# VectorE's weight roundings in two parts, weights used one step later, and one plain token chunk in place of two, in a fused attention and MLP kernel

## The chip, the cores and the metric

The kernel runs on one core of a Trainium2 chip. The metric is the time of one execution on the device, in microseconds (us). Engines are named as the profile names them: PE is TensorE, PEld its weight loads, DVE is VectorE, ACT ScalarE, POOL GpSimd, SP SyncE. A ratio is the mean time of one kernel's fast runs over the mean of the other kernel's fast runs in the same rounds, so it is not quite the ratio of the medians that are quoted beside it. Below 1 is faster than the kernel before.

## The reference, cut to what matters

```python
def _attn_ref(q, k, v, tau):                      # q, k, v: (8, 8, 576, 64)
    scores = scale * np.matmul(q, k.transpose(0, 1, 3, 2))
    thresh = np.max(scores, axis=-1, keepdims=True) - tau
    scores = np.where(scores >= thresh, scores, -1000000000.0)
    attn = np.exp(scores - np.max(scores, axis=-1, keepdims=True))
    attn = attn / (np.sum(attn, axis=-1, keepdims=True) + 1e-09)
    return np.matmul(attn, v)

def _moe_ref(x, w_in, w_out):                     # x: (4608, 512), d_ff 2048
    r = np.maximum(x @ w_in, 0.0)
    return (r * r) @ w_out
```

The weights arrive as 64-bit floats and are rounded to 32 bits on the chip. That is the work that the change moves.

## The kernel before

Work goes in *steps*. A step takes one block of 128 query rows of a pair of heads: scores on TensorE (L200), the row maximum on VectorE (L205), exponentials on ScalarE (L216), the masks on VectorE (L228), the division on GpSimd (L240), and for blocks of earlier steps transposes and the product with v on TensorE. VectorE works in the order in which the program issues. There are two score buffers, and the masks free them, so TensorE's next scores wait for masks.

Weights come in 32 *pieces* of rounding (16 of w_in, 16 of w_out). One piece takes two operations on ScalarE, three on VectorE and two on GpSimd:

```python
        elif stage == 1:
            nc.vector.tensor_scalar(out=tu, in0=hi, scalar1=0x80000000, ...)          # L137
            nc.vector.scalar_tensor_tensor(out=tu, in0=eu, scalar=3, in1=tu, ...)     # L138
            nc.vector.tensor_scalar(out=eu, in0=tu, scalar1=0xFF800000, ...)          # L140
        elif stage == 2:
            nc.gpsimd.tensor_tensor(out=d, in0=d, in1=e, op=ALU.mult)                 # L142
        else:
            nc.gpsimd.tensor_tensor(out=weight_piece(i)[1], in0=..., in1=..., op=ALU.add)   # L144
```

The plan of how many pieces each step rounds is the following; from step 20 on, `i == NBLK` is every fifth step: 24, 29, 34.

```python
        if s < HP * FIRST:                        # steps 0 to 7
            x = int(n > 0 and i == 0)
        else:
            x = 2 if n >= 2 * HP and i == NBLK else 1
```

In a step the order on VectorE is maximum, `round_weights(now[0], 1)` (L137, L138, L140), masks; in the last step of a pair of heads (24, 29 and 34 among them) the next q and k are transposed before the masks, and the rounding stands behind the masks. A second piece of the same step runs whole at the end of the step, in front of the next step's maximum.

TensorE fills its time between attention parts with *pieces* of the MLP, one of 1.76 us by the program's count, taken from a queue as soon as the weights they need are rounded:

```python
    def fill(us):
        state["left"] += us
        while waiting and state["left"] >= PIECE_US / 2 and waiting[0][0] <= state["rounded"]:
            ...                                   # issue the piece
```

The MLP runs on 18 chunks of 256 tokens. The first two (`PLAIN = 2`) use 16 plain output pieces each (L399, 4 records a piece); all later ones use seven products in 14 pieces (L431), which multiply with sums of quarters of w_out. The 16 subtractions that make these sums (L390, VectorE) stand one behind each input piece of chunk 2:

```python
        if j == PLAIN:
            posts.append(lambda: sum_quarters(x))
```

Their slots are the same memory in which raw weights are staged and the third slot of attention weights lies. The last rounding is in step 34, and the program lets no sum be made before step 37.

## Time and profile before

| | kernel before |
|---|---|
| time, median of 3 runs | 1431.7 us (1430.45 to 1433.82) |
| profiled execution | 1435.75 us, span 1434.0 us |
| TensorE idle in the whole span | 50.6 us |
| TensorE's waits, 100 to 250 us | 15.2 us, 7.0 of them for the last rounding (L144) |

The table of stretches for three stretches; the columns are the stretch, its length, the busy time of PE, PEld, DVE, ACT, POOL with instruction counts, the granted TensorE clock, the DMA share and GB/s:

```profile
20.00:60.00 40.00, 34.40 (x229) 25.49 (x230) 31.87 (x73) 23.56 (x59) 20.88 (x29) 0.87 0.64 124
100.00:250.00 150.00, 134.75 (x932) 89.68 (x932) 118.16 (x226) 87.17 (x210) 109.53 (x125) 0.94 0.39 100
250.00:440.00 190.00, 188.44 (x942) 133.90 (x941) 120.23 (x249) 53.95 (x135) 94.34 (x125) 1.00 0.47 86
```

Between 100 and 250 us, where most weights are rounded, TensorE is idle for 15.25 us and its clock is 0.94. From 250 us on it is idle for 1.56 us.

### The profile page before, as it was taken

The page shows a single profiled execution, that of the slowest core. Times are in us where ns is not written, and L with a number is a line of the kernel's source. Part 1 is how long each engine was busy: PE and PEld are TensorE (multiplying, and loading weights), DVE is VectorE, ACT ScalarE, POOL GpSimd, SP SyncE. Part 2 cuts the span into 40 slices and gives each one's busy share as a digit, 9 for nine tenths or more (in the row PEclk, how much of TensorE's full clock was granted, in tenths as well). Part 3 has the DMA queues.
Part 4 walks back from the last instruction along what each step waited for, and adds up shares of the span by engine and source line. Part 5 has one row for each costly group of instructions (what it writes and reads, how often), then busy time and mean ns, then how long its engine had stood idle before and what let it go on. Part 6 is the DMA issues. An engine that isn't in the chain of part 4 may idle for free.

```text
span 1434.0 us, 21996 instructions
## 1 busy us (share of the span) xinstructions
PE 1383.4 (96%) x7412; PEld 1055.1 (74%) x7412; DVE 853.3 (60%) x1770; ACT 435.5 (30%) x1064; POOL 708.4 (49%) x928
## 2 busy tenths in 40 slices
PE   5899988999999999999999999999999999999998
PEld 3676555747787777777777777778777777788887
DVE  5898875557756665756665657566657566621011
ACT  3765654323222323232222222223223232210100
POOL 3688766426454545354545435555454354531321
PEclk9999999999999999999999999999999999999999
DMA  7554442345544554454545544544555545430000
GB/s 149 126 139 122 111 103 53 63 78 102 91 91 92 106 101 93 79 106 88 98 87 106 96 91 89 105 87 91 91 109 89 94 87 104 77 73 15 1 15 15
DMA packets 503823, 125.93 MB, mean 88 GB/s; under 512 B 494912, under 2 KB 495712, under 8 KB 503712
## 3 DMA queue, kind: packets, MB, share of 16 engines
q1 hardware_dynamic: 494448, 107.42, 40.8%
q0 software_dynamic: 6880, 16.82, 3.8%
q8 instruction: 60, 0.98, 0.3%
q10 hardware_dynamic: 2384, 0.30, 0.1%
q14 instruction: 51, 0.42, 0.1%
HBM read 48.63 MB, written 9.44 MB: 40 GB/s over the span
## 4 chain that ended last, share of the span: by engine, by line
PE 86%; DVE 7%; issue 2%; ACT 2%; POOL 2%; DMA 1%; SPq 1%; DVEq 0%; POOLq 0%; ACTq 0%
PE bank L368 35%; PE bank L431 23%; PE s L200 12%; PE bank L319 11%; PE bank L399 3%; DVE w L228 1%; DVE st L205 1%; DVE turned L138 1%; PE bank L258 1%; DVE turned L137 1%; DVE turned L289 1%; ACT wT L259 1%; DVE turned L140 0%; DVE wo L228 0%; DMA wo<-in_moe_w_in_dram 0%
## 5 line engine op out<-in xcount | busy, mean ns | idle before, releaser
L368 PE MATMUL bank<-xT,w_in_sb 128*128 128x256 f32 x2304 | 521.4, 383 | 1.8 <-ACT osb L406 1.2
L368 PEld LDWEIGHTS bank<-xT,w_in_sb 128*128 128x128 f32 x2304 | 433.1, 190 | 82.7 <-issue 21.3
L205 DVE TENSOR_REDUCE st<-s 128x1 f32<-128x576 f32 x288 | 206.9, 753 | 323.5 <-PE s L200 323.3
L240 POOL TENSOR_SCALAR w<-w,st 128x576 f32<-128x576 f32 x269 | 236.6, 887 | 28.6 <-DVE st L231 22.1
L228 DVE SCALAR_TENSOR_TENSOR w<-s,st,w 128x576 f32<-128x576 f32 x269 | 207.5, 804 | 72.1 <-ACT w L216 72.0
L431 PE MATMUL bank<-wo,gsum 128*128 128x256 f32 x1024 | 234.0, 381 | 1.4 <-DVE u_sum L446 1.4
L379 POOL TENSOR_TENSOR g<-g 128x512 f32<-128x512 f32 x144 | 149.6, 1040 | 155.2 <-ACT g L378 131.5
L431 PEld LDWEIGHTS bank<-wo,gsum 128*128 128x128 f32 x1024 | 192.6, 190 | 36.4 <-issue 7.2
L200 PE MATMUL s<-kT,qT 64*128 64x288 f32 x1024 | 175.9, 439 | 27.3 <-DVE w L228 10.2
L238 POOL TENSOR_SCALAR st<-st 128x2 f32<-128x2 f32 (+1 forms) x160 | 38.0, 238 | 324.6 <-DVE w L228 311.2
L216 ACT ACTIVATE w<-s,st 128x576 f32<-128x576 f32 x269 | 184.9, 733 | 0.2 <-ACT st L214 0.2
L319 PE MATMUL bank<-wT,vs 128*64 128x128 f32 (+3 forms) x1700 | 178.6, 358 | 4.1 <-ACT wT L259 3.4
L431 PE MATMUL bank<-wo,g 128*128 128x256 f32 x768 | 178.7, 383 | 2.1 <-DVE osb L450 2.1
L431 PEld LDWEIGHTS bank<-wo,g 128*128 128x128 f32 x768 | 143.8, 190 | 31.6 <-issue 8.2
L200 PEld LDWEIGHTS s<-kT,qT 64*128 64x128 f32 x1024 | 99.4, 190 | 91.4 <-issue 66.6
L289 DVE STREAM_TRANSPOSE turned<-w 128x576 f32<-128x576 f32 x225 | 162.1, 754 | 3.5 <-POOL w L240 3.5
L319 PEld LDWEIGHTS bank<-wT,vs 128*64 128x64 f32 x1700 | 105.4, 140 | 74.8 <-issue 23.2
L378 ACT ACTIVATE g<-bank 128x512 f32<-128x512 f32 x144 | 86.2, 599 | 200.8 <-PE bank L368 200.8
L213 ACT ACTIVATE st<-st 128x2 f32<-128x2 f32 (+1 forms) x160 | 33.3, 208 | 324.9 <-DVE st L205 324.1
L333 ACT COPY xT<-bank 128x256 f32<-128x256 f32 x42 | 15.6, 372 | 279.8 <-PE bank L319 279.8
L444 DVE TENSOR_TENSOR gsum<-g 128x512 f32<-128x512 f32 x32 | 20.8, 681 | 107.3 <-PE bank L431 107.3
L399 PE MATMUL bank<-wo,g 128*128 128x512 f32 x128 | 62.1, 620 | 7.3 <-POOL wo L144 7.0
(69 smaller groups left out, 944.6 us busy)
## 6 DMA issues: line engine op xcount, KB each, us to landing
wT<-turned SPq DMA_DIRECT2D x800, 72.0 KB, 2.2
ql<-in_q_dram SPq DMA_DIRECT2D x126, 72.0 KB, 2.5
wo<-in_moe_w_in_dram SPq DMA_DIRECT2D x16, 512.0 KB, 4.7
wo<-in_moe_w_out_dram SPq DMA_DIRECT2D x16, 512.0 KB, 3.7
out_dram<-osb POOLq DMA_DIRECT2D x32, 256.0 KB, 2.7
vs<-in_v_dram POOLq DMA_DIRECT2D x50, 128.0 KB, 3.5
kl<-in_k_dram SPq DMA_DIRECT2D x63, 72.0 KB, 2.5
kl<-in_k_dram SPq DMA_DIRECT2D x63, 64.0 KB, 2.3
```

Source lines behind the costliest of these rows:

```text
L200: nc.tensor.matmul(sc[u][:, half, 0:HALF], lhsT, kT[rows, half * HALF:(half + 1) * HALF], start=True, stop=True)
L205: nc.vector.tensor_reduce(out=mx[:, u:u + 1], in_=sc[u][:, :, 0:HALF], axis=AX.XY, op=ALU.max)
L216: nc.scalar.activation(out=w[:, u, :].rearrange("p (h k) -> p h k", h=2), in_=sc[u][:, :, 0:HALF], func=AF.Exp, bias=bias[:, u:u + 1], sca ...
L228: nc.vector.scalar_tensor_tensor(out=wu, in0=sc[u][:, :, 0:HALF], scalar=thr[:, u:u + 1], in1=wu, op0=ALU.is_ge, op1=ALU.mult, accum_out=s ...
L240: nc.gpsimd.tensor_scalar(out=w[:, u, :], in0=w[:, u, :], scalar1=z[:, u:u + 1], scalar2=rcp[:, u:u + 1], op0=ALU.add, op1=ALU.mult)
L289: nc.vector.transpose(wb[:, u * KB:(u + 1) * KB, i % 2, :], w[:, u, :].rearrange("p (k q) -> p k q", q=32))
L319: nc.tensor.matmul(ps[u * D:(u + 1) * D, 0:nq], vs[n % 2][:, u * (NBLK + 1) + c, :], wT[:, cw, cols], start=(c == 0), stop=(c == NBLK))
L368: nc.tensor.matmul(h[:, x % 2, :], w_in_sb[:, c, f * P:(f + 1) * P], xT[:, c, at:at + TCH], start=(c == 0), stop=(c == NMC - 1))
L378: nc.scalar.activation(out=to, in_=h, func=AF.Relu)
L379: nc.gpsimd.tensor_tensor(out=to, in0=to, in1=to, op=ALU.mult)
L399: nc.tensor.matmul(o[t].rearrange("p (h d) -> p h d", h=2), g[:, f, t * P:(t + 1) * P], mov, start=(f == 0), stop=(f == NFT - 1))
L431: nc.tensor.matmul(to, left[:, f, :], wo[:, slot, f, :], start=(f == 0), stop=(f == HF - 1))
```

## The change

Its intent is threefold. *Split*: the third VectorE operation of a rounding (L140) goes behind the masks, so that the masks, which free the score buffers, come earlier. *Delay*: a rounded weight counts as usable only from the next step on, so that TensorE doesn't stand waiting for it. *Products*: `PLAIN = 1`, so chunk 1 too is done in 14 product pieces; the sums it needs are then made in steps 37 to 39. Cut to its core (asserts, the renumbered stages and the bodies of unchanged functions are left out):

```diff
+        elif stage == 2:
             nc.vector.tensor_scalar(out=eu, in0=tu, scalar1=0xFF800000, scalar2=None, op0=ALU.bitwise_and)
-        elif stage == 2:
+        elif stage == 3:
             nc.gpsimd.tensor_tensor(out=d, in0=d, in1=e, op=ALU.mult)
@@ mlp_in
-        if j == PLAIN:
-            posts.append(lambda: sum_quarters(x))
+        if j == PLAIN and state["step"] > first_dma + 1:
+            posts.append(lambda: some_sums(2))
@@ product
+        if sums:
+            some_sums(16 if x > 1 else 8)
@@
-    PLAIN = 2
+    PLAIN = 1
@@ fill
-        while waiting and state["left"] >= PIECE_US / 2 and waiting[0][0] <= state["rounded"]:
+        while waiting and state["left"] >= PIECE_US / 2 and waiting[0][0] <= state["usable"]:
@@ the loop over steps
+        state["usable"] = rounded_by[-1]
+        rounded_by.append(state["rounded"])
@@ before the masks
                 round_weights(now[0], 1)
-                round_weights(now[0], 2)
@@ behind the masks
+            if now:
                 round_weights(now[0], 2)
+                round_weights(now[0], 3)
```

## The prediction

> **What bounds the kernel now.** I read the page first, then the table of TensorE's waits, then the table of stretches, then the timeline around the longest waits. On the page, parts 1, 2 and 5:
>
> ```profile
> PE 1383.4 (96%) x7412; PEld 1055.1 (74%) x7412; DVE 853.3 (60%) x1770; ACT 435.5 (30%) x1064; POOL 708.4 (49%) x928
> PE   5899988999999999999999999999999999999998
> ...
> PEclk9999999999999999999999999999999999999999
> ...
> L399 PE MATMUL bank<-wo,g 128*128 128x512 f32 x128 | 62.1, 620 | 7.3 <-POOL wo L144 7.0
> ```
>
> TensorE is busy for 1383.4 of 1434.0 us, so all idle time together is 50.6 us, and most of it lies in the first seven or eight slices, while weights are being rounded. No change of waits alone can make 2% (28.6 us) unless it empties that stage. What TensorE waits for in the whole trace:
>
> ```profile
> PE s L200 <- DVE w L228: 11.9, 9, 3.5
> PE s L200 <- DVE kT L179: 9.3, 3, 8.4
> PE s L200 <- DVE wo L228: 7.7, 5, 3.0
> PE bank L399 <- POOL wo L144: 7.0, 5, 2.6
> ```
>
> Scores (L200) wait for VectorE's masks (L228), because the masks free the two score buffers: 19.6 us. Output products (L399) wait for freshly rounded weights (L144): 7.0 us. The table of stretches prices a long wait further:
>
> ```profile
> core 0: us, PE busy (x) PEld busy (x) DVE busy (x) ACT busy (x) POOL busy (x), PEclk, DMA share, GB/s
> 198.00:202.40 4.40, 1.78 (x15) 1.06 (x13) 4.26 (x6) 1.91 (x6) 4.10 (x5) 0.93 0.88 254
> 202.40:208.80 6.40, 6.40 (x27) 3.53 (x28) 4.97 (x9) 1.27 (x3) 5.46 (x6) 0.52 0.91 183
> 133.00:142.00 9.00, 9.00 (x34) 6.65 (x36) 8.08 (x15) 3.15 (x8) 7.03 (x9) 0.62 0.78 169
> ```
>
> After the 2.62 us wait at 199.8 us the clock is 0.52 for 6.4 us, so another 6.4 x 0.48 = 3.1 us is lost. After the 1.73 us wait at 131.3 us it is 0.62 for 9 us: 3.4 us. After the 2.12 us wait at 170.1 us the same view gives 0.77 for 7.3 us: 1.7 us. The three cost 8.2 us of work beyond their own length.
>
> **What sets a step while weights are rounded.** From the timeline at 219 us:
>
> ```profile
> 218.64 1.27 POOL L144 TENSOR_TENSOR wo<-turned 128x512 f32<-128x512 f32 x1
> 218.72 1.47 DVE L137 TENSOR_SCALAR turned<-wo 128x512 uint32<-128x512 uint32 x1
> 220.30 0.69 DVE L138 SCALAR_TENSOR_TENSOR turned<-turned 128x512 uint32<-128x512 uint32 x1
> 221.03 0.43 DVE L140 TENSOR_SCALAR turned<-turned 128x512 uint32<-128x512 uint32 x1
> 221.37 0.81 DVE L228 SCALAR_TENSOR_TENSOR w<-s,st,w 128x576 f32<-128x576 f32 x1
> 221.60 1.28 POOL L142 TENSOR_TENSOR turned<-turned 128x512 f32<-128x512 f32 x1 [1.69 <-DVE turned L140]
> ```
>
> L137 takes 0.42 us alone and 1.47 us here, ending just after GpSimd's L144. The masks start when L140 is through. Seen from the end M of the masks: L144 ends at M+3.5, L137 at M+3.8, L138 at M+4.6, L140 at M+5.0, the next masks at M+6.6. L142 starts at 215.12, 221.60 and 228.07 us, 6.5 us apart: a closed loop of VectorE and GpSimd, and TensorE, with 5.9 to 6.2 us of work in such a step with one MLP piece, is only just as long.
>
> **What the Trainium skill says.** "SBUF — State Buffer", section "SBUF: two separate sides": a VectorE operation with two SBUF inputs or in a two-port mode and a GpSimd operation exclude each other for the whole instruction. The trace agrees for L137 and L138 against L142 and L144 (0.42 to 1.47 us, 0.69 to 1.58 us). [...]the weight sums (L390) have a median of 0.68 us where the one-tensor L140 of as many elements takes 0.43. "TensorE: Matmul & The Clock Gate", section "Part 1: The HAM clock gate": after an idle window of about 3.4 us the array runs at half rate. The trace shows the half rate, but after holes of 1.7 to 2.6 us; the 1.66 us hole at 238.6 us did not trip it. The measured holes are what I use.
>
> **The change, part by part.**
>
> (a) *Chunk 1 by seven products.* The bookkeeping of the program, followed by hand, gives 14 product pieces for 16 plain output pieces. A plain piece is 4 records, and the chain has x16 in 7.06 us, so 16 pieces take 28.3 us. The chain has 112 records of L431, one chunk's 14 pieces, in 24.17 us, up to 24.8 where interrupted. Saved: 28.3 - 24.5 = 3.8 us of TensorE work. All of it is on the path.
>
> (b) *L140 after the masks.* 32 instructions leave the stretch between maximum and masks. The masks then need the exponentials and L138 only. In the new loop L140 runs at M+0.4, L142 ends at M+2.2, L240 at M+4.1, L144 at M+5.4; L137 starts at M+2.5 and no longer meets L144; the exponentials end at M+4.2 and the masks at about M+5.7. The loop falls from 6.5 to 5.7 us, below TensorE's step. Of TensorE's waits for masks I take off what L140, or L138 held by GpSimd, added at each: 0.4 at 39.7 us, 0.4 at 61.9, 0.8 at 68.0, 0.3 at 78.5, 0.9 at 133.0, 1.4 at 172.2, 0.4 at 222.3. Sum 4.6 us. The first waits (3.5, 3.0 and 2.1 us) have no rounding in front of them and stay.
>
> (c) *Weights a step later.* The five waits on L144 (7.0 us) and the one of L368 (0.6) go. But the 2.62 us one lies in step 30, where the second rounding of step 29 holds the maximum back to 200.33 us and the masks can't end before about 206: it comes back as a wait for masks. Net 5.0 us. Against that, the bookkeeping shows fewer pieces to fill holes: none in steps 17 and 21 (before: 1 and 3), one in most of the rest; at the end of step 35 31 pieces are done (before 36), then 12 come at once in step 36. The late pieces are not lost, since TensorE runs without a break afterwards, but holes open: step 17 has 4.3 us of work in a 5.7 us loop (1.4 us), step 21 has 3.4 us (2.3 us). New: 3.7 us.
>
> (d) *The sums of weights.* Before, 16 subtractions were spread over six steps of chunk 2. In the changed order 4 stand in front of step 38's maximum, 2 between it and the masks, and 10 in one row in front of step 39's. Step 38: I get masks about 1.0 us after TensorE wants them. Step 39: from the end of step 38's masks 0.35 + 10 x 0.68 + maximum 0.76 + two transposes 1.43 + mask 0.82 + 0.35 + the transposes of q and k 1.5 = 12.0 us until the next scores can start; TensorE has 1.0 us of scores and 4 pieces of 1.78, with the start 7.4 us after those masks. Hole: 4.6 us. Sum 5.6 us.
>
> (e) *Clock.* Before 8.2 us. After, long holes in steps 21, 30 and 39, some 3 us each: 9.0. Change +0.8.
>
> Sum: -3.8 - 4.6 - 5.0 + 3.7 + 5.6 + 0.8 = -3.3 us; 1431.7 - 3.3 = 1428.4, say 1428.5 us.
>
> **Rivals.** *Sums cost nothing* (TensorE is late enough in steps 37 to 39, or the throttle lets the hole pass): then -3.3 - 5.6 - 3 = -12 us, 1420. For it: before, step 44 holds three sums and TensorE waits only 0.40 us. Against: there they were three, here ten. *The holes of the delay win*: if steps 17, 20, 21 and 30 each lose a clock window and GpSimd, whose L240 now starts 1.5 us later after the masks, makes the transposes wait (before, the transposes waited for GpSimd hardly at all), 6 us more: 1434 to 1436. For it: GpSimd is 88% busy from 100 to 140 us. *TensorE hides all of it*: from 250 us on it has no idle time worth naming (4.2 us in 400 to 1200), so only (a) counts: 1428.
>
> **Range and chances.** The terms that could go wrong are (d) with its share of (e), about 8 us, and the holes of (c), about 6 us; in quadrature with a spread of runs of 1430.45 to 1433.82 this gives some 8 us to either side. The floor of all idle time makes 2% faster (1403) nearly impossible, and 2% slower (1460) would need a stall that nothing here shows.
>
> **What would show it.** Right: L399 x64 and L431 x1904 records; no wait on L144 over 0.5 us; L142's starts about 6 us apart in place of 6.5; a hole of TensorE for kT or masks of 3 to 5 us behind the row of ten sums, with a lowered clock after it; busy time of TensorE 3 to 4 us down except for clock. Wrong: no hole there (then faster, near 1420), or waits of L258 for GpSimd's L240 (then slower), or L140 in its new place meeting L142 of another piece and holding the next maximum.

## More of the kernel before

The profiled execution is slower than all three timed ones.

In the first stretch the clock was 0.87 in this execution: 40 x 0.13 = 5.2 us of clock.

Line numbers after the first hunk are one higher in the changed kernel, later ones up to seven: L200 is L201, L228 is L229, L140 is L141, L142 is L143, L144 is L145, L240 is L241, L390 is L393, L399 is L403, L431 is L438. In the variants with a changed choice of PSUM banks L403 is L406 and L438 is L441.

## The result, and the profile after

The changed kernel takes 1437.62 us (median of 4 runs, 1437.34 to 1438.55). The kernel before took 1431.43 us in the same rounds. The ratio is 1.0042, 95% interval 1.0024 to 1.0059: slower by 0.4%. That is within the 2% that the prediction was nearly certain of, but outside its range (1428.5 with some 8 us to either side, so about 1420 to 1436), and of the opposite sign. The output is correct.

From the page of the changed kernel, part 1:

```profile
PE 1378.8 (96%) x7460; PEld 1064.8 (74%) x7460; DVE 857.1 (60%) x1781; ACT 435.8 (30%) x1063; POOL 722.2 (50%) x933
```

TensorE works 4.6 us less than before (1378.8 against 1383.4) and the span is 1.9 us longer, so it is idle for 57.1 us, 6.5 us more. The same three stretches as above:

```profile
20.00:60.00 40.00, 33.91 (x239) 24.96 (x239) 32.65 (x74) 24.59 (x61) 20.89 (x29) 0.91 0.66 128
100.00:250.00 150.00, 134.65 (x945) 91.36 (x942) 118.82 (x236) 88.96 (x215) 116.50 (x128) 0.94 0.39 101
250.00:440.00 190.00, 183.23 (x965) 141.77 (x965) 120.65 (x242) 49.41 (x121) 97.36 (x125) 0.99 0.44 81
```

Two things are read from it. In the stage of the roundings nothing was won: 15.25 us of idle time before, and now 15.35, with the same clock of 0.94. And from 250 to 440 us, where there was hardly any idle time, there are 6.77 us in place of 1.56. What TensorE waits for from 100 to 250 us in the changed kernel (line and waiter, releaser, us in total, times, longest us):

```profile
PE s L201 <- DVE w L229: 7.5, 4, 3.9
PE s L201 <- DVE wo L229: 2.9, 1, 2.9
PE bank L403 <- ACT g L379: 2.0, 1, 2.0
PE bank L369 <- ACT osb L410: 1.6, 1, 1.6
```

In the kernel before the same view had 7.0 us for the last rounding (L144; the line stands in the prediction), 4.2 us for masks and nothing long for ScalarE:

```profile
PE s L200 <- DVE w L228: 2.1, 2, 1.7
PE s L200 <- DVE wo L228: 2.1, 1, 2.1
```

Now no wait for the rounding is left, as the delay intends, and 10.4 us for masks (7.5 + 2.9; wo is the third slot of attention weights, which lies in that memory) and 3.6 us for ScalarE stand in its place. The idle time changed its name.

(A hole is named by the step whose masks the scores of the next step wait for.) Where it is longest, in step 30, the timeline of VectorE in the changed kernel reads (start us, us, engine, line, operation):

```profile
195.84 0.82 DVE L229 SCALAR_TENSOR_TENSOR w<-s,st,w 128x576 f32<-128x576 f32 x1 [0.24 <-ACT w L217]
...
199.45 0.47 DVE L137 TENSOR_SCALAR turned<-wo 128x512 uint32<-128x512 uint32 x1
200.02 1.58 DVE L138 SCALAR_TENSOR_TENSOR turned<-turned 128x512 uint32<-128x512 uint32 x1
201.63 0.43 DVE L141 TENSOR_SCALAR turned<-turned 128x512 uint32<-128x512 uint32 x1
201.98 1.41 DVE L206 TENSOR_REDUCE st<-s 128x1 f32<-128x576 f32 x2
...
205.86 0.81 DVE L229 SCALAR_TENSOR_TENSOR w<-s,st,w 128x576 f32<-128x576 f32 x1
```

And TensorE's at the same place:

```profile
206.82 1.77 PE L201 MATMUL s<-kT,qT 64*128 64x288 f32 x4 [3.92 <-DVE w L229]
```

Step 29 rounds two pieces, both behind its masks; the first one's operations (196.97 to 199.54) are left out at the first "...". The three of the second piece (199.45 to 202.06) come on top, between the masks of step 29 (195.84) and the maximum of step 30 (201.98). From masks to masks it takes 10.0 us, and TensorE, with one MLP piece in the step, stands still for 3.92 us. From 206 to 212 us its clock is 0.50. Step 25, behind step 24 with two pieces, looks alike (2.95 us).

The second new hole, in the timeline of the changed kernel, VectorE, GpSimd and TensorE:

```profile
279.39 10.00 DVE L393 TENSOR_TENSOR wo<-wo 128x512 f32<-128x512 f32 x10
279.65 4.42 POOL L241 TENSOR_SCALAR w<-w,st 128x576 f32<-128x576 f32 x2 [0.26 <-DVE st L232]
285.58 1.59 POOL L358 TENSOR_TENSOR gsum<-g 128x512 f32<-128x512 f32 x1
287.23 5.35 PE L438 MATMUL bank<-wo,gsum 128*128 128x256 f32 x16 [4.08 <-POOL gsum L358]
294.10 1.24 PE L201 MATMUL s<-kT,qT 64*128 64x288 f32 x8 [1.52 <-DVE kT L180]
```

The ten sums in a row take 1.00 us each in the mean; the median of all 16 is 0.68. Beside them GpSimd's two divisions take 4.42 us; two of them took 1.63 us elsewhere (at 216.31 us). So GpSimd's sum of g (L358) is late, TensorE waits 4.08 us for it, and another 1.52 us for the transposed k, which VectorE reaches only behind the row.

The part that worked is seen in steps 32 to 35. VectorE's timeline of the changed kernel:

```profile
220.17 0.81 DVE L229 SCALAR_TENSOR_TENSOR w<-s,st,w 128x576 f32<-128x576 f32 x1
...
222.05 0.41 DVE L141 TENSOR_SCALAR turned<-turned 128x512 uint32<-128x512 uint32 x1
```

L141 now follows the masks, and the next step's masks start at 225.60 us, 5.4 us later, where the loop took 6.5 us before.

**How far the difference of 6 us is real.** Fifty-three executions of the kernel before were timed. They lie between 1430.31 and 1436.18 us, with a mean of 1433.0. The records of the 49 of them that list a clock order them:

| mean granted clock of the execution | executions | mean time |
|---|---|---|
| 0.990 to 0.991 | 10 | 1435.5 us |
| 0.993 to 0.995 | 25 | 1432.9 us |
| 0.996 to 0.999 | 14 | 1431.7 us |

The four that stand beside the changed kernel were on the quick side (mean 1431.8). Against the mean of all 53 the changed kernel, whose four runs have a clock of 0.990 to 0.992, is 4.8 us slower, or 0.33%. So 1.2 us of the 6 come from which executions of before were caught, and a comparison of the two profiled executions (1434.0 and 1435.9 us) shows only 1.9 us, since the profiled one of before was one of its slowest.

### The profile page after: what moved, and what is told of

Same layout as the page of the kernel before. It is cut to its first block, busy times and chain, and to the rows that moved or that the text cites. A ratio compares the mean times of both kernels' runs of the same rounds, so it can differ in the third digit from the quotient of the medians.

```text
span 1435.9 us, 22123 instructions
## 1 busy us (share of the span) xinstructions
PE 1378.8 (96%) x7460; PEld 1064.8 (74%) x7460; DVE 857.1 (60%) x1781; ACT 435.8 (30%) x1063; POOL 722.2 (50%) x933
## 4 chain that ended last, share of the span: by engine, by line
PE 79%; DVE 9%; SPq 5%; issue 3%; ACT 2%; DMA 1%; POOL 1%; DVEq 0%; POOLq 0%; ACTq 0%
PE bank L369 33%; PE bank L438 22%; PE s L201 12%; PE bank L320 10%; DVE w L229 2%; SPq L301 2%; SPq L308 2%; PE bank L403 2%; DVE st L206 1%; PE bank L259 1%; DVE turned L138 1%; DVE turned L290 1%; DVE wo L393 1%; SPq L162 1%; ACT w L217 1%
## 5 line engine op out<-in xcount | busy, mean ns | idle before, releaser
L438 PE MATMUL bank<-wo,gsum 128*128 128x256 f32 x1088 | 251.8, 384 | 5.8 <-POOL gsum L358 4.5
L241 POOL TENSOR_SCALAR w<-w,st 128x576 f32<-128x576 f32 x269 | 241.1, 904 | 27.4 <-DVE st L232 19.6
L229 DVE SCALAR_TENSOR_TENSOR w<-s,st,w 128x576 f32<-128x576 f32 x269 | 207.6, 804 | 75.8 <-ACT w L217 75.7
L438 PEld LDWEIGHTS bank<-wo,gsum 128*128 128x128 f32 x1088 | 205.3, 191 | 45.8 <-issue 9.6
L201 PE MATMUL s<-kT,qT 64*128 64x288 f32 x1024 | 178.6, 441 | 38.3 <-DVE w L229 17.2
L438 PE MATMUL bank<-wo,g 128*128 128x256 f32 x816 | 189.5, 382 | 0.9 <-DVE osb L457 0.9
L438 PEld LDWEIGHTS bank<-wo,g 128*128 128x128 f32 x816 | 153.1, 190 | 30.5 <-issue 6.9
L201 PEld LDWEIGHTS s<-kT,qT 64*128 64x128 f32 x1024 | 101.3, 191 | 95.8 <-issue 66.6
L334 ACT COPY xT<-bank 128x256 f32<-128x256 f32 x42 | 15.7, 373 | 281.4 <-PE bank L320 281.4
L184 POOL COPY qmid<-qT 64x64 f32<-64x64 f32 x64 | 18.3, 286 | 103.7 <-DVE qT L180 101.8
```

What stands on the lines that cost most here:

```text
L201: nc.tensor.matmul(sc[u][:, half, 0:HALF], lhsT, kT[rows, half * HALF:(half + 1) * HALF], start=True, stop=True)
L229: nc.vector.scalar_tensor_tensor(out=wu, in0=sc[u][:, :, 0:HALF], scalar=thr[:, u:u + 1], in1=wu, op0=ALU.is_ge, op1=ALU.mult, accum_out=s ...
L241: nc.gpsimd.tensor_scalar(out=w[:, u, :], in0=w[:, u, :], scalar1=z[:, u:u + 1], scalar2=rcp[:, u:u + 1], op0=ALU.add, op1=ALU.mult)
L438: nc.tensor.matmul(to, left[:, f, :], wo[:, slot, f, :], start=(f == 0), stop=(f == HF - 1))
```

## The experiments

Each kernel ran in five rounds beside the kernel before on the same chip. The sittings were on different chips (15, 8, 5, 3 and again 8), so kernels of different sittings are compared by their ratios. Times are medians. Except where said, outputs were correct. "Idle" and "clock lost" are of TensorE from 100 to 250 us unless said; clock lost is the sum over stretches of 10 us of length times one minus the granted clock.

### First round: each part alone

**e0_before**: the kernel before, unchanged, as a check on the comparison and for a second profile.

> The kernel before, unchanged, for a second profile and for the noise. All theories: ratio 1.000 within 0.001. Its first profile was of an execution of 1435.75 us where the timed ones have a median of 1431.4; a second profile near 1431 should show which waits of the first were of that one execution only. If the first profile was typical, TensorE waits 19.6 us for masks and 7.0 us for rounded weights again.

Measured: 1434.15 us, ratio 0.9997 (0.9982 to 1.0012). Its profiled execution has a clock of 1.00 in the stretch from 20 to 60 us, where the first profile of the same kernel had 0.87; idle 15.4 us and 8.5 us of clock lost from 100 to 250 us are the same in both. What follows: the clock of the first 60 us is luck of the execution, up to 5.2 us, and profiles are to be compared stage by stage.

**e1_split**: the changed kernel with the split alone.

```diff
-    PLAIN = 1
+    PLAIN = 2                                          # and sums one per piece, in chunk 2, as before
-        while waiting and ... waiting[0][0] <= state["usable"]:
+        while waiting and ... waiting[0][0] <= state["rounded"]:
```

> Only the third VectorE instruction of a rounding is moved behind the masks; weights are used at once and two chunks are summed the plain way, as before. Theory A (the split is good, the loss is elsewhere): 3 to 5 us faster, 1427 to 1428, with less waiting of TensorE for masks. Rival (the split itself costs: GpSimd's first multiplication starts later and finished weights with it): TensorE's wait for rounded weights grows from 7 to over 12 us and the time is the same or up to 4 us longer.

Measured: 1440.78 us, ratio 1.0051 (1.0033 to 1.0069): slower, by the rival's way and by more than its 4 us. Of TensorE's waits in the whole trace the first line is now:

```profile
PE bank L403 <- POOL wo L145: 13.1, 8, 2.6
```

Waits for masks fell by 1.9 us only (17.7 in place of 19.6), and waits for the rounded weight rose from 7.0 to 13.1 us. What follows: with the third VectorE operation behind the masks, GpSimd's two operations of the same piece start later, and a kernel that uses a weight as soon as it counts as rounded waits for it. The split is a loss without the delay.

**e2_delay**: the delay alone.

```diff
-    PLAIN = 1
+    PLAIN = 2                                          # and sums as before
@@ before the masks
                 round_weights(now[0], 1)
+                round_weights(now[0], 2)
+                round_weights(now[0], 3)
@@ behind the masks
-            if now:
-                round_weights(now[0], 2)
-                round_weights(now[0], 3)
```

(in the branch behind the masks, steps that lay out the next q and k keep theirs there, as in the kernel before).

> Only the use of rounded weights is a step later. Theory A (the delay loses a little by itself, since pieces that filled TensorE's waits for masks come later, and much only with the sums): 1 to 4 us slower; the 7 us of waits for rounded weights vanish and waits for masks grow by as much or more. Rival B (the holes of the delay are the whole loss): 6 us slower or more, the same as the changed kernel. Rival C (prediction: the delay gains 1 us or so): 1 to 3 us faster.

Measured: 1439.45 us, ratio 1.0043 (1.003 to 1.0057): slower, as much as rival B had said. No wait for a rounding is left, but of all waits the first is now:

```profile
PE s L201 <- DVE w L229: 20.7, 15, 4.2
```

Together with the line for the third slot of attention weights (10.3 us) TensorE waits 31.0 us for masks, 11.5 more than in e0. The long ones are 2.78 us at 140.95 us (step 21), 4.36 us at 177.24 us (step 25) and 4.15 us at 212.81 us (step 30).

**e3_products**: products alone.

```diff
-        while waiting and ... waiting[0][0] <= state["usable"]:
+        while waiting and ... waiting[0][0] <= state["rounded"]:
@@ the split undone as in e2_delay
```

> Only chunk 1 is summed by the seven products, with weights used at once and roundings in one part. The chunk's pieces then stand in steps 35 to 39 and the 16 sums of weights are spread over steps 37 to 39 between them rather than ten in a row. Theory A: 2 to 4 us faster, from 3.8 us less TensorE work, with no hole of over 2 us behind the sums. Rival D (the products in chunk 1 cost by themselves, since sums and GpSimd's work on the squares collide in any order): 2 to 4 us slower, with the hole of 4 us at the second product again.

Measured: 1435.05 us, ratio 1.0009 (0.9996 to 1.0022), and a **wrong** result (relative error 0.25). By the program's own order the cause is that, without the delay, pieces of chunk 1 run in steps 35 and 36, where they take PSUM bank 5 while the old way of transposing still uses banks 4 and 5; this is argued, not shown. Its time says little; the question is asked again below with a correct kernel.

### Second round: pairs, and the row of sums

**e5_delay_products**: the changed kernel without the split (undone as in e2_delay).

> The changed kernel with the rounding in one part again (delay and products kept). Theory E (where weights are used a step later, the split takes some 4.5 us off the waits for masks: 31.0 us in the delay alone, 26.5 us in the changed kernel): 2 to 5 us slower than the changed kernel, ratio to before 1.006 to 1.008. Rival (the split costs in any company, as it did alone): faster than the changed kernel, ratio under 1.003.

Measured: 1447.03 us, ratio 1.0094 (1.0081 to 1.0108), slower than theory E had it. Against the changed kernel (1.0042) the split is thus worth 0.0052 x 1433 = 7.5 us where the delay is there. Alone it cost 7 us.

**e6_split_delay**: split and delay, without the products.

```diff
-    PLAIN = 1
+    PLAIN = 2                                          # and sums one per piece, in chunk 2, as before
```

> The changed kernel with two plain chunks again (split and delay kept). Theory E (the products save 3.8 us of work but open holes of about 5.6 us behind the sums and a half-clock stretch of 1.7 us): 2 to 4 us faster than the changed kernel, ratio to before 1.001 to 1.003. Rival (the products pay even so): ratio 1.006 to 1.008.

Measured: 1431.6 us, ratio 0.9989 (0.9977 to 1.0002), faster than either expectation. Two parts, each of which costs 0.4 to 0.5% alone, are together a gain of 0.1% that can't be told from none. From 100 to 250 us it has the same waits as the changed kernel, 14.8 us idle and 8.6 us of clock lost. The kernel before has 15.2 and 8.6 us there, so split and delay together won nothing in that stage; in the profile e6's idle time is lower only from 440 to 1300 us (1.7 us against 4.2). The rest of the changed kernel's loss, 6 us between the medians and 7.6 by the ratios, belongs to the products and their sums.

**e7_spread**: the changed kernel, with the sums one behind each piece in place of rows of 4, 2 and 10.

```diff
-            posts.append(lambda: some_sums(2))
+            posts.append(lambda: some_sums(1))
-            some_sums(16 if x > 1 else 8)
+            some_sums(1)                               # and the order FT1, FT2, FT3, FT4, in which they are read
```

> The changed kernel with the 16 sums of weights one at a time, between the pieces of chunk 1, in the order in which the products read them, in place of ten in a row. Theory E (the row of ten holds GpSimd's squares and VectorE's masks): the holes of 4.1 and 1.5 us at 283 and 292 us go, and the time falls by 5 to 7 us, to ratio 0.999 to 1.001. Rival (the burst of twelve pieces in step 36 makes the squares late anyway): the hole at the second product stays, over 3 us, and the time falls by under 2 us.

Measured: 1433.05 us, ratio 0.9998 (0.9984 to 1.0012). The row itself costs (1.0042 - 0.9998) x 1433 = 6.3 us. But e7 is still 1.4 us slower than e6, which has no products in chunk 1 at all. The saving of the products doesn't show.

**e8_products_spread**: products alone, sums spread, and chunk 1 kept from banks 4 and 5 in the early steps.

```diff
-            used["h"] = take("mm", (6, 7)) if j < PLAIN else bank[ring3[pair % 3]]
+            used["h"] = (take("mm", (6, 7)) if j < PLAIN or state["step"] <= first_dma + 2
+                         else bank[ring3[pair % 3]])    # and split and delay undone, sums spread as in e7
```

> Chunk 1 by the products alone, with weights used at once and roundings in one part, the sums one per piece, and the first pieces of chunk 1 in two other PSUM banks until the transposes have left bank 5 (the kernel with the products alone gave a wrong result, I think since a transpose wrote into a half-filled bank). Theory E: correct, and 3 to 6 us faster than before, ratio 0.996 to 0.998, since the 3.8 us of work come off and the holes behind the sums don't open. Rival (sums beside GpSimd's squares cost in any order): ratio 1.000 to 1.002 as with the sums in pairs.

Measured: 1432.06 us, ratio 0.9997 (0.9985 to 1.001), not the 0.996 to 0.998 expected, and **wrong** again (relative error 0.073). By the program's order the switch from one rule of banks to the other put two pairs of chunk 1 into bank 6 one after the other, the second before the first was read. That the choice of banks was the cause, e13 shows; the pairs are read from the program.

### Third round: roundings spread evenly, and correct banks

The traces pointed at the steps that round two pieces. The next kernels round one piece in two more of the early steps and never two:

```diff
-            x = int(n > 0 and i == 0)
+            x = int(n > 0 and (i == 0 or n < 3))
-            x = 2 if n >= 2 * HP and i == NBLK else 1
+            x = 1
```

This *even* plan does two things at once: no step has a second piece, and the weights are two pieces ahead from step 8 to 23 and one from 24 to 28, so that TensorE has MLP pieces in steps 17, 20 and 21 that were empty in e6. In step 30 TensorE has one piece in both plans, and in the four steps before it five in both, so that step tells the two effects apart.

**e10_even**: e6_split_delay with the even plan.

> Split and delay with two plain chunks, as in the run e6_split_delay (1431.6 us, ratio 0.9989), but the roundings spread evenly: no step rounds two pieces; the eleven of a step pair are spread so that each step from the eighth on has at most one. Theory: the second piece's three VectorE operations stand before the next step's maximum in steps 24 and 29, so the masks of steps 25 and 30 come late, TensorE has holes of about 3 and 4 us there and a half clock after them. Then e10 is 2 to 6 us faster than e6, ratio 0.995 to 0.998, and the holes of steps 25 and 30 fall under 1.5 us each. Rival: TensorE just has too few pieces in those steps; the holes stay above 2.5 us and the ratio is about 0.999.

Measured: 1419.06 us, ratio 0.9897 (0.9882 to 0.9911), 1% faster than the kernel before and more than was expected. TensorE's waits from 100 to 250 us begin with

```profile
PE bank L320 <- ACT wT L260: 2.2, 9, 0.2
PE s L201 <- DVE w L229: 1.2, 4, 0.6
```

and all idle time there is 5.7 us in place of 14.8, with a clock of 1.00 in place of 0.94. Step 30 in the timeline, VectorE:

```profile
192.78 1.42 DVE L206 TENSOR_REDUCE st<-s 128x1 f32<-128x576 f32 x2
194.11 0.48 DVE L137 TENSOR_SCALAR turned<-wo 128x512 uint32<-128x512 uint32 x1
194.69 0.69 DVE L138 SCALAR_TENSOR_TENSOR turned<-turned 128x512 uint32<-128x512 uint32 x1
195.31 0.81 DVE L229 SCALAR_TENSOR_TENSOR w<-s,st,w 128x576 f32<-128x576 f32 x1
```

The masks of step 29 started at 189.25 us, so from masks to masks it is 6.1 us, not 10.0, and the scores that waited 3.92 us in the changed kernel start at 196.77 us without any wait. With the same TensorE work in these steps, the second piece is shown to be the cause of the hole in step 30. For steps 17, 20, 21, 23 and 25 it isn't told apart whether it is that or the earlier pieces.

**e11_even_products**: all of the change, with sums spread as in e7, the even plan, and banks by the parity of the pair.

```diff
-            used["h"] = take("mm", (6, 7)) if j < PLAIN else bank[ring3[pair % 3]]
+            if j == PLAIN and pair < 6:
+                used["h"] = bank[6 + pair % 2]
+            else:
+                used["h"] = take("mm", (6, 7)) if j < PLAIN else bank[ring3[pair % 3]]
```

> All of the change (one plain chunk), with the sums one per piece, the roundings even as in e10 and the PSUM banks of chunk 1 taken by parity of the pair. Theory: e10 plus what the products are worth once the row of sums is gone, 0 to 2 us: ratio 0.994 to 0.998. Rival: the products cost TensorE's waits as much as they save or more: 1 us slower than e10. The outputs should be correct.

Measured: 1418.84 us, ratio 0.9896 (0.9881 to 0.991). Against e10 the products are worth 0.2 us, which is nothing that these runs can tell from zero.

**e12_before_even**: the kernel before with the even plan alone.

> The kernel before with the even roundings alone, neither split nor delay. If two pieces in one step are what makes holes in general, 1 to 4 us faster than before (ratio 0.997 to 0.9995). Rival: in the kernel before the late weights (waits of 7 us at the projections for GpSimd's finished piece) and the masks (19.6 us) remain, and there is no gain: ratio 1.000 within 0.001.

Measured: 1428.27 us, ratio 0.9963 (0.995 to 0.9976), a little more than expected. The plan alone gives 5 us.

**e13_products_fixed**: products alone, sums spread, with the banks of e11.

> The products alone, with sums one per piece, as e8_products_spread, but with the PSUM banks of chunk 1 chosen so that nothing is overwritten. It should be correct, and as fast as e8: ratio 0.998 to 1.0005 (e8 0.9997), as the products are worth nothing in time by themselves. Rival: the wrong banks of e8 hid a wait, and correct ones cost over 2 us: ratio over 1.001.

Measured: 1430.3 us, ratio 0.9985 (0.9969 to 1.0002), correct. Only the choice of banks differs from e8, so it was the cause of the wrong result. In time it can hardly be told from e8 or from the kernel before.

### Fourth round: what stayed open

**e15_even_split** and **e16_even_delay**: the even plan with one of the two parts.

> Even roundings and split, without the delay, two plain chunks. With e12 (even alone, 0.9963) and e10 (even, split and delay, 0.9897) it tells whether the split needs the delay also when no step rounds two pieces. Theory: yes, since the split makes each finished weight later by the masks' time, so the output products wait for GpSimd's last rounding as in e1_split (13 us): slower than e12, ratio 0.999 to 1.003. Rival: the two-piece steps caused those waits: ratio 0.991 to 0.996.

> Even roundings and delay, without the split, two plain chunks. Theory: without the two-piece steps the delay leaves few holes, but the loop of a step stays at 6.5 us, so the masks still make TensorE wait (31 us in e2_delay, 24 to 27 here): ratio 0.994 to 0.997, 6 to 10 us slower than e10. Rival 1: the two-piece steps were the whole trouble, and e16 is as fast as e10, 0.990. Rival 2: the delay needs the split whatever the steps hold: slower than before, 1.002 to 1.004.

Measured: e15 1428.24 us, ratio 0.9964 (0.9948 to 0.9979); e16 1425.22 us, ratio 0.995 (0.9936 to 0.9964). e16 lies where its theory put it; e15 lies just beyond the rival's range, neither as slow as the theory said nor as fast as the rival. The eight kernels without products read

| ratio to the kernel before | neither | split | delay | both |
|---|---|---|---|---|
| two-piece steps | 0.9997 | 1.0051 | 1.0043 | 0.9989 |
| even plan | 0.9963 | 0.9964 | 0.9950 | 0.9897 |

In either row the two parts together are better than the sum of the two. With the even plan the split gives nothing without the delay (three waits for L145, 6.9 us, the longest 3.67) and 0.0053 x 1433 = 7.6 us with it. So the two-piece steps are a cause and not the whole of it: the split needs the delay, whatever the steps hold.

**e17_after_even**: the changed kernel with the even plan and the banks of e11, its sums in rows.

> The changed kernel with the even roundings and the PSUM banks of chunk 1 by parity; the sums still stand in rows of 4, 2 and 10 (or as the pieces now fall). Theory: the row of sums costs about 4 us by the wait for GpSimd's difference and 1 to 2 us for the transposes, as in the change itself: 4 to 7 us slower than e11, ratio 0.9925 to 0.9945. Rival: with fewer holes before, TensorE is late enough there to hide it: within 2 us of e11, ratio 0.989 to 0.991.

Measured: 1425.11 us, ratio 0.9949 (0.9937 to 0.9962), 0.0053 x 1433 = 7.6 us slower than e11 with spread sums. The even plan alone thus turns the changed kernel from 0.4% slower into 0.5% faster. That is close to the size that the theory gave (0.9945), but not by its way: the row's cost is here one wait for the transposed k and none for GpSimd. TensorE's timeline:

```profile
278.46 2.29 PE L201 MATMUL s<-kT,qT 64*128 64x288 f32 x8 [7.86 <-DVE kT L180]
```

**e14b_sums_late**: e11 with the sums made in chunk 2, as in the kernel before, and chunk 1's products reading finished weights in their place. Its output is wrong, which doesn't matter for the time.

```diff
-        if j == PLAIN and state["step"] > first_dma + 1:
+        if j == 2:
-        if sums:
+        if sums and j > PLAIN:
+        if j == PLAIN:
+            slot = {FT1: Q00, FT2: Q01, FT3: Q10, FT4: Q11}.get(slot, slot)
```

> As e11_even_products (1418.8 us, ratio 0.9896), but the 16 sums of weights are made in chunk 2, one behind each piece, where the kernel before makes them; chunk 1's products read finished weights of another quadrant in place of the sums: a wrong result on purpose. Theory: the sums stand in front of masks and transposes in steps 36 to 39 and give back as idle time (2.6 us between 250 and 440 us, and 1.7 us of clock) what the products save. Then e14b is 2 to 4 us faster than e11 and e10, ratio 0.987 to 0.988. Rival: the chain of the products through GpSimd's and VectorE's differences of g makes the holes; then e14b is within 1 us of e11, ratio about 0.9893.

Measured: 1415.96 us, ratio 0.9878 (0.986 to 0.9897), 2.9 us less than e11 and 3.1 us less than e10 by the medians. The intervals of the ratios overlap, but the runs themselves don't: e14b's four lie between 1415.52 and 1416.57 us, those of e10 and e11 between 1418.58 and 1419.37 (on another chip; the kernel before had medians of 1433.32 and 1433.85 beside them). The largest wait of TensorE from 250 to 440 us, e11 first:

```profile
PE s L201 <- DVE kT L180: 2.7, 2, 2.3
```

and e14b, where it is the only one:

```profile
PE s L201 <- DVE kT L180: 0.8, 1, 0.8
```

All idle time in that stretch is 3.5 us in e11 and 0.9 in e14b, and e11 loses 1.7 us of clock there, e14b none. So, as far as two sittings on two chips can tell, the products do save close to 3 us, and the sums, standing in front of VectorE's transposes in steps 37 to 39 even when spread, give it all back.

Of the correct kernels e10_even and e11_even_products, 1% faster than the kernel before and by the medians 1.3% faster than the changed one, are the best; e10 is the simpler.

## Why the prediction was wrong, point by point

The step that failed most is (c), and with it the sum in which (b) and (c) stand as independent gains; (a) and (d) come next.

The miss is 1437.6 - 1428.5 = 9.1 us. By the parts, roughly: (b) and (c) together were to give -5.9 us, and e6 gives -1.6 (0.0011 x 1433); (a), (d) and (e) together were to cost 2.6 us, and cost 6.0 between the medians of e6 and the changed kernel. Those are 4.3 and 3.4 us of it. The prediction counted from 1431.7 us where the mean of before is 1433.0; that makes the remaining 1.3.

**(a), the products: the saving was over-sized, and "all of it is on the path" failed.** Chunk 1's records do L403 x64 and L438 x1904, as said. Between e10 and e11 TensorE's busy time at L403 and L438 (the groups' busy times added) falls from 472.6 to 469.7 us: 2.9 us, not 3.8; e14b shows the same 3 us as time. But in every kernel whose sums stand in chunk 1 it comes out as zero (e11 against e10, 0.2 us) or less (e7 against e6, 1.4 us slower). The saving and the sums are one bargain, and the prediction had booked only the long row as its cost.

**(b), the third operation behind the masks: the loop shortened as described, but the part was taken as independent, and it isn't.** Loops of 5.2 to 6.0 us from masks to masks in steps 32 to 35, L141 behind the masks and no masks wait there are as predicted. The 4.6 us are not: the split alone cost 7 us (e1), because the finished weight comes later too, which the prediction worked out (L144 at M+5.4 in place of M+3.5) and then didn't charge since (c) took it away. With the delay it is worth 7.5 us (e5 against the changed kernel), more than predicted. Of its seven places three came off (68.0 us: from 1.65 to 0.80; 133.0: from 1.73 to 0.67; 222.3: from 0.39 to none). The one at 39.7 fell from 1.33 to 0.94, but was 0.80 in e0 without any change; the one at 61.9 stayed at 0.8; and two grew: 78.5 from 0.32 to 1.04, and 172.2, in step 25, from 2.12 to 2.95. Before 100 us, where 1.9 us were to come off, all waits for masks together went from 15.1 to 15.7 us (15.3 in e1). Why isn't known: no run isolates those steps.

**(c), weights a step later: this is the step that failed most; the holes that the delay opens were under-sized.** The waits for L144 went, as said. The holes that came in their place were put at 3.7 us beside a returned 2.62; the lines of the changed kernel are 1.97 us in step 17 (predicted 1.4), 0.67 and 0.97 us in steps 20 and 21 (2.3), 2.01 us in step 23 for ScalarE's relu (none), 2.95 us in step 25 (none) and 3.92 us in step 30 (2.62). Together that is 12.5 us, where the prediction's terms leave 7.8: 1.4 + 2.3 + 2.62, and 0.8 and 0.7 us of the old waits of steps 20 and 25 that (b) had not taken off. The prediction saw in step 30 that "the second rounding of step 29 holds the maximum back". It didn't see that step 24 does the same to step 25, nor ask whether the plan of the roundings should be the thing to change. e10 shows that it was: with the plan alone changed, idle time from 100 to 250 us falls from 14.8 to 5.7 us and the lost clock from 8.6 us to nothing.

**(d), the row of sums: nearly right in size, wrong in the way.** Ten sums were taken as 6.8 us and took 10.0. TensorE's new waits are 4.08 + 1.52 = 5.6 us, the very number predicted, but most of it is for GpSimd's sum of g, slowed by the same row, and not for the transposed k, and the 1.0 us of step 38 did not come: that the sums agree is luck. In e17, where the row falls otherwise, it is 7.86 us for k alone. Counted by the runs, the row costs 6.3 us (e7) to 7.6 us (e17), against 5.6 and a share of the clock.

**(e), the clock: near in its sum, by luck.** From 100 to 250 us the changed kernel loses 8.5 us, and 1.7 us more behind the row; predicted 9.0 us in all. But the places were to be steps 21, 30 and 39, and they are step 23 (1.7 us), 25 and 30 (3.4 us each) and 39 (1.7 us); step 21 lost nothing.

**The rivals.** "The holes of the delay win" (1434 to 1436) was the true one in direction. It named lost clock windows in steps 17, 20, 21 and 30, of which only that of step 30 came, and transposes that wait for GpSimd's division, which did not come at all. So that it lies within 2 to 4 us of the measured time is luck too. What it missed are the two-piece steps and the sums' share. "Sums cost nothing" is refuted by e7, e14b and e17, and "TensorE hides all of it" by the idle time from 250 to 440 us, 6.77 us in place of 1.56.

**The range.** The prediction adds terms of 8 and 6 us in quadrature to "some 8 us". The root of 64 + 36 is 10, without the spread of runs; with that the range would have ended at 1438.5 us, just above the measured time. A smaller slip: by its own lines the next masks end at M+6.5, not M+6.6.

**What stays open.** The changed kernel has 2.9 us more idle time than e6 from 440 to 1300 us (4.6 us against 1.7; waits of 1.6 us for k and 1.4 us for a product's sum are in it), in a stage that the change doesn't touch but for when pieces come; e10 (4.0) and the kernel before (4.2) have more there than e6, too. No run isolates it. And it isn't told which half of the even plan, no second pieces or earlier ones, ends the holes of steps 17, 20, 21, 23 and 25.

## What to carry to other kernels

Two edits on one loop, here when a value is made and when it is used, can each lose alone and win together; price them as a pair, and test the pair and each half. Before moving operations inside a step, look for the steps that hold double the work: one irregular step in five undid the whole gain of split and delay, and an even plan, two lines, turned it from none into 1%. A saving on the bound engine must be booked together with the work on other engines that it calls for, at the place in their queues where that work will stand.

## What the Trainium skill lacked or had wrong

- "TensorE: Matmul & The Clock Gate", section "Part 1: The HAM clock gate", has half rate begin after one idle window of about 3.4 us; further down, under "A second HAM failure mode: psum-queue depth-cycling", it lets frequent short idles do it too, but without a length. Here the clock was 0.51 from 171.40 to 178.00 us, behind a hole of 2.95 us, and no hole of 3.4 us was needed; but behind one of 1.97 us at 114.02 us it stayed at 1.00, and in e10 it fell to 0.50 behind two holes of 1.45 and 1.43 us that lie 6 us apart. The length of one hole doesn't decide. The table of stretches of e10 (the holes end at 39.97 and 45.87 us) and of the changed kernel:

```profile
48.00:52.00 4.00, 4.00 (x27) 3.14 (x26) 3.70 (x7) 2.49 (x6) 2.92 (x4) 0.50 0.84 195
```

```profile
171.40:178.00 6.60, 6.56 (x20) 4.24 (x21) 5.45 (x12) 2.38 (x6) 5.20 (x6) 0.51 0.96 156
```

- The same section's window of 3.4 us does agree with the sizes: the lost clock of all traces comes in multiples of 1.7 us (1.7, 3.4, 5.1, 8.5), which is half a window each. It says that the slow start of a kernel varies from run to run and stays under 1% of a typical span. What it lacks is how much the half rate in the middle of a kernel is worth between executions of one kernel: 53 executions of the kernel before spread over 5.9 us, and those with a clock of 0.990 to 0.991 are 3.8 us longer in the mean than those with 0.996 to 0.999.
- "SBUF — State Buffer", section "SBUF: two separate sides", has VectorE's operation with two SBUF inputs and a GpSimd operation that reads SBUF shut each other out for the whole instruction. The direction agrees (sums 1.00 us in the mean in place of 0.68, divisions 2.21 us in place of 0.82), the size does not add up: strictly in turn, ten sums, two divisions (0.82 each), one square (1.04) and two sums of g (1.27 each) would take 6.8 + 1.6 + 1.0 + 2.5 = 12.0 us, and VectorE's row beside them took 10.0. That is an estimate from single durations elsewhere in this trace (0.68 is the median); if it holds, a part of each recorded duration lies outside the exclusion. The page gives no way to price a row.
